# First eight units of a recurrent attention and feed-forward kernel: loads, state copies and hand order rearranged

## The chip, the core and the metric

The kernel runs on one core of a Trainium2 chip. The metric is the time of one execution on the device in microseconds (us). One execution was also recorded by the hardware profiler; its own span, from the first to the last instruction, is a little shorter than the time that is reported for it.

## What is computed

The first half is a linear recurrence per batch and head (4 batches, 8 heads, 768 steps, head size 48). The second half is a feed-forward block with a SiLU over all 3072 tokens (384 to 2048 to 384). All inputs and the output are 32-bit floats.

```python
for t in range(S):
    cur = np.einsum('bhd,bhe->bhde', u[None] * kt, vt)
    y[:, :, t] = np.einsum('bhd,bhde->bhe', rt, state + cur)
    state = w[None, :, :, None] * state + np.einsum('bhd,bhe->bhde', kt, vt)
...
h = x @ w_in
g = h * (1.0 / (1.0 + np.exp(-h)))
return (g @ w_out)
```

## The kernel before

**Units and stages.** The 768 steps are cut into 6 chunks of 128. A unit is one chunk of one batch: 24 units, numbered with the batch running fastest, so units 0 to 3 are the first chunk, units 4 to 7 the second. For a unit the kernel loads r, k and v (one request each of 192 KB, `ld`), transposes r and k on TensorE (`turn`, letter T, into one of two PSUM tiles `att`), multiplies them on VectorE with powers of w (`rT` and `kT`), forms the products of all pairs of steps (`product`, A; two units at once from unit 4 on, `product_pair`, A45), masks them on VectorE (`masked`, am), multiplies with v (`outputs_y`, Y, of which y16 is the sum with the bonus term on VectorE) and brings y into transposed form (yT on TensorE, xT on ScalarE). The bonus term is made on GpSimd (ku, ru, vu) with one sum on VectorE (rd).

**The state.** Between chunks a state per batch is kept twice, in 32 bits (`st`) and in 16 bits (`st16`, shown as stb). `outputs_s` (S) makes a chunk's contribution in a PSUM tile `sp`. In the first chunk, `state` only copies it out, in two halves of 48 rows each, each half once as stb and once as st. In later chunks VectorE adds it to the decayed old state (`decayed_state`, sd, on GpSimd), and `state16` (stb) makes the 16-bit copy on GpSimd. `decayed_k` (kc, GpSimd) is what S reads.

**Feed-forward.** When the units of a chunk are done, w_in is applied in pieces (`l1_mm`, L, into a PSUM tile `hps`, and `l1_silu`, G, on ScalarE) and then w_out (`l2_mm`, into `ops`). A piece of chunk 0 has six multiplications and ends in one G of 512 columns. The word L2.8 means: the pair of batches that starts at 2, columns of w_in from 128 times 8 on. H0 to H3 are such pieces of chunk 1. The tiles hps, sp, yp, yT and ops share four PSUM slots; a new one waits for the oldest to be read.

**What sets the order.** Nothing is rescheduled: each engine runs its instructions in the order in which the program writes them, and waits on semaphores where it needs another engine's result. For the first eight units this order is a list of words in the string `order`, worked off from left to right: a letter and a unit, such as T4, kT4, st1, or a number and a star in front, such as 10*T0, which puts that many idle multiplications (`spin`) on TensorE ahead of the step. lnw, eK and lamK make the powers of w, mx makes the second mask (`cross_mask`), i_q and i_o request quarters of w_in and w_out from GpSimd's queue. After the list a loop takes units 6 and 7, then 8 and 9, and so on, and puts pieces of feed-forward work (`fill`) between their steps.

**First loads.** Requests go out on the queues of SyncE (SP) and ScalarE (ACT) in program order. Ahead of the list stand w in two parts, u spread over all rows (`u_bc`), w as a row (`w_row`), and r, k and v of units 0 to 3; v of unit 0 and k of unit 1 go out on ACT, the others on SP.

Of the kernel before, what the change touches and what calls it, by code (L numbers as in the profile page):

```python
# [15 lines left out]
def kernel(  # L16
# [11 lines left out]
    nc = tc.nc  # L28

    B, H, S, D = r.shape  # L30
    C = 128
# [10 lines left out]
    HC = C // 2  # L42
# [7 lines left out]
    def unit(i):  # L50
        return divmod(i, B)
# [10 lines left out]
    rin = [big.tile([128, H, 64], FP, name=f"rin{i}") for i in range(NIN)]  # L62
    kin = [big.tile([128, H, 64], FP, name=f"kin{i}") for i in range(NIN)]
    vin = [big.tile([128, H, D], FP, name=f"vin{i}") for i in range(NIN)]
# [6 lines left out]
    def ld(i, dst, src, eng=nc.sync):  # L71
        sc, b = unit(i)
        eng.dma_start(
            out=dst[i % NIN][:, :, 0:D],
            in_=src[b, :, sc * C:sc * C + C, :].rearrange("h t d -> t h d"))

    def load(i):
        if i >= NU:
            return
        for dst, src in ((rin, r), (kin, k), (vin, v)):  # L80
            ld(i, dst, src)
# [11 lines left out]
    def columns(eng, dst, src, j):  # L93
        eng.dma_start(out=dst[64 * j:64 * j + D, :],
                      in_=bass.AP(tensor=src.tensor, offset=D * j, ap=[[1, D], [PW, NP]]))
# [6 lines left out]
    nc.vector.memset(idle, 0.0)  # L102
    columns(nc.sync, wpT, w, 1)
    columns(nc.scalar, wpT, w, 0)
    nc.scalar.dma_start(out=u_bc, in_=bass.AP(tensor=u.tensor, offset=0,
                                              ap=[[0, 128], [D, H], [1, D]]))
    nc.scalar.dma_start(out=w_row, in_=bass.AP(tensor=w.tensor, offset=0, ap=[[0, 1], [1, HD]]))
    for i in range(B):
        for dst, src in ((rin, r), (kin, k), (vin, v)):
            by_act = (i == 0 and dst is vin) or (i == 1 and dst is kin)  # L110
            ld(i, dst, src, nc.scalar if by_act else nc.sync)
    nc.vector.memset(ones, 1.0)
    for i in range(B):
        nc.vector.memset(rin[i][:, :, D:64], 0.0)
# [1 line left out]
    for b in range(B):  # L116
# [10 lines left out]
    maskM = cst.tile([128, C], FP)  # L127
    nc.gpsimd.memset(maskM, 1.0)
    nc.gpsimd.affine_select(
        out=maskM, in_=maskM, compare_op=ALU.is_ge, fill=0.0,  # L130
# [3 lines left out]
    maskX = cst.tile([128, C], FP)  # L134
# [6 lines left out]
    eK = cst.tile([PR, NP, C], FP)  # L141
    lamR = cst.tile([PR, NP, C], FP)
    lamK = cst.tile([PR, NP, C], FP)
    lnw_bc = cst.tile([128, HD], FP)
    lamC = cst.tile([128, H, D], FP)
# [39 lines left out]
        nc.scalar.preload_act_table_set("silu_and_others")  # L185

    def cross_mask():
        nc.scalar.copy(out=maskX[0:HC, :], in_=maskM[HC:C, :])
        nc.scalar.copy(out=maskX[HC:C, :], in_=maskM[0:HC, :])

    live = {}

    def L(i):
        return live.setdefault(i, {})

    def bonus_products(i):
        bonus_ku(i)
        bonus_rku(i)
# [10 lines left out]
    def decayed_k(i):  # L209
        nc.gpsimd.tensor_tensor(out=kc[i % NIN][:, :, 0:D], in0=kin[i % NIN][:, :, 0:D],  # L210
                                in1=lamC, op=ALU.mult)

    def bonus_sum(i):
        L(i)["rku"] = wrk.tile([128, H], FP, name="rku")
        nc.vector.tensor_reduce(out=L(i)["rku"], in_=L(i)["rku_f"],  # L215
                                axis=mybir.AxisListType.X, op=ALU.add)

    def bonus_v(i):
        L(i)["vu"] = wrk.tile([128, H, D], FP, name="vu")
        nc.gpsimd.tensor_tensor(out=L(i)["vu"], in0=vin[i % NIN],  # L220
                                in1=L(i)["rku"].unsqueeze(2).broadcast_to([128, H, D]),
                                op=ALU.mult)

    def crossed(i):
        return i >= B and i % 2 == 1
# [47 lines left out]
    def product_pair(i):  # L273
        a = [next_att().rearrange("p j (g c) -> p j g c", g=NP) for _ in range(2)]
        for e in range(2):
            L(i + e)["a"] = a[e]
        for s0, c0 in ((0, 0), (HC, HC)):
            for p in range(NP):
                for e in range(2):
                    rT, kT = L(i + e)["rT"], L(i + e)["kT"]  # L280
                    o0 = s0 if e == 0 else HC - s0
                    for j, r0 in ((0, 0), (1, 64)):
                        nc.tensor.matmul(a[e][o0:o0 + HC, j, p, c0:C],  # L283
                                         kT[r0:r0 + D, p, s0:s0 + HC],
                                         rT[r0:r0 + D, p, c0:C],
                                         start=True, stop=True)

    def masked(i):
        am = L(i)["am"] = wrk.tile([128, 2, NP, C], F16, name="am")
        nc.vector.tensor_tensor(  # L290
            out=am.rearrange("p h g c -> p (h g) c"), in0=L(i)["a"].rearrange("p h g c -> p (h g) c"),
            in1=(maskX if crossed(i) else maskM).unsqueeze(1).broadcast_to([128, H, C]), op=ALU.mult)
# [27 lines left out]
    def outputs(i):  # L320
        outputs_y(i)
        outputs_s(i)

    def decayed_state(i):
        sc, b = unit(i)
        if 0 < sc < NCH - 1:
            L(i)["sdec"] = wrk.tile([PR, NP, PW], FP, name="sdec", bufs=4)
            nc.gpsimd.tensor_tensor(out=L(i)["sdec"], in0=st[b],  # L328
                                    in1=wCT.unsqueeze(2).broadcast_to([PR, NP, PW]), op=ALU.mult)

    def evict_y(i):
        L(i)["y16"] = wrk.tile([128, H, D], F16, name="y16")
        nc.vector.tensor_tensor(out=L(i)["y16"], in0=L(i)["y"], in1=L(i)["vu"], op=ALU.add)  # L333

    def state(i):
        sc, b = unit(i)
        if sc == NCH - 1:
            return
        sps = L(i)["sps"]
        for p0, c0 in ((0, 0), (64, D)):  # L340
            dst = st[b][p0:p0 + D, :, c0:c0 + D]
            src = sps[p0:p0 + D, :, c0:c0 + D]
            if sc:
                nc.vector.tensor_tensor(out=dst, in0=src,
                                        in1=L(i)["sdec"][p0:p0 + D, :, c0:c0 + D], op=ALU.add)
            else:
                nc.scalar.copy(out=st16[b][p0:p0 + D, :, c0:c0 + D], in_=src)  # L347
                nc.scalar.copy(out=dst, in_=src)

    def state16(i):  # L350
        sc, b = unit(i)
# [74 lines left out]
    def fill(n):  # L426
        for _ in range(n):
            if fillers:
                fillers.pop(0)()
# [14 lines left out]
    def piece(word, f):  # L444
# [16 lines left out]
        "lr": lambda i: ld(i, rin, r), "lk": lambda i: ld(i, kin, k), "lv": lambda i: ld(i, vin, v),  # L461
    }
    order = """
        lnw eK lamK pads lr4 lk4 lv4 lr5 lk5 lv5 lr6 lk6 lv6 lr7 lk7 lv7 10*T0 ku0 kT0 rT0 v160
        ru0 5*A0 rd0 ku1 am0 T1 wb v161 ru1 lnwb lamC kT1 rT1 1*Y0 vu0 rd1 T2 i_q0 y160 A1 vu1
        yT0 xT0 v162 ku2 am1 kT2 rT2 ru2 4*Y1 y161 2*A2 yT1 xT1 i_q1 rd2 vu2 v163 T3 am2 ku3 kT3
        rT3 Y2 L0.0 y162 ru3 A3 i_q2 L0.2 G0.0 yT2 G0.2 xT2 rd3 am3 vu3 kc0 Y3 L0.4 G0.4 y163
        kc1 L0.6 G0.6 yT3 kc2 S0 st0 xT3 i_q3 kc3 L2.0 G2.0 L2.2 G2.2 S1 st1 L2.4 G2.4 L2.6 G2.6
        ku4 mx S2 st2 L0.8 G0.8 L0.10 G0.10 S3 st3 ru4 T4 kT4 rT4 v164 r164 L2.8 G2.8 L2.10
        G2.10 rd4 ku5 i_o0 vu4 T5 kT5 rT5 r165 v165 A45 ru5 kc4 sd4 L0.12 G0.12 am4 L0.14 G0.14  # L470
        am5 kc5 rd5 vu5 sd5 Y4 S4 y164 L2.12 G2.12 st4 Y5 S5 y165 L2.14 G2.14 st5 yT4 xT4 stb4
        stb5 i_o1 T6 kT6 rT6 yT5 xT5 ku6 ru6 i_o2 kc6 v166 r166 H0 H1 H2 T7 kT7 rT7 i_o3 H3 r167
        v167 ku7 ru7 kc7 sd6 sd7
    """
    for word in order.split():
        if "*" in word:
            n, word = word.split("*")
# [18 lines left out]
    for i in range(B + 2, NU, 2):  # L496
        sc, b = unit(i)
        nxt = range(i + 2, min(i + 4, NU))
        product_pair(i)
        if i > B + 2:  # L500
            for n in nxt:
                bonus_products(n)
                decayed_k(n)
        masked(i)
        masked(i + 1)
        if i == B + 2:
            for n in (i, i + 1):
                bonus_sum(n)
                bonus_v(n)
            for n in nxt:  # L510
                bonus_products(n)
                decayed_k(n)
        fill(4)
        outputs(i)
        evict_y(i)
        turn_y_dma(i)
        state(i)
        state16(i)
        fill(2)
        outputs(i + 1)  # L520
        evict_y(i + 1)
        turn_y_dma(i + 1)
        state(i + 1)
        state16(i + 1)
        if b:
            fillers.extend((first(sc) if sc > 1 else rest_first(sc)) + second(sc))
        fill(2)
        for n in nxt:
            turn(n)
            decay(n)  # L530
        load(i + B)
        load(i + 1 + B)
        for n in nxt:
            bonus_sum(n)
            cast_v(n)
            bonus_v(n)
            decayed_state(n)
        for n in nxt:
            fill(2)
            cast_r(n)  # L540
        fill(4)
# [31 lines left out]
```

## Time and profile before

| what | value |
|---|---|
| time, median of 3 runs | 198.1 us (198.0 to 199.08) |
| the profiled execution | 198.3 us, span 196.6 us |
| PE busy | 182.9 us, 93% of the span |
| POOL, ACT, DVE busy | 120.5, 109.8, 97.8 us |
| granted TensorE clock, mean | 0.998 |
| first product of unit 0 on PE | starts at 9.02 us |
| first w_out work on PE (L407) | starts at 52.07 us |

PE is TensorE, PEld its weight loads, DVE is VectorE, ACT is ScalarE, POOL is GpSimd, SP is SyncE. A row of a timeline gives the start in us, the length in us, the engine, the line of the kernel, the operation, output and inputs, shape and count; in brackets stands how long the engine was idle before and what released it. A row of the chain of waits gives start, length and what the end was waiting for. In the chain of waits, PE has 76% of the span, each other engine 6% or less.

### The profile page before, as it was taken

How to read it: one execution, taken by the hardware profiler on the slowest of the kernel's cores; microseconds unless marked ns; L12 is line 12 of the kernel's file. 1: busy time of each engine (PE TensorE's matmuls, PEld its weight loads, DVE VectorE, ACT ScalarE, POOL GpSimd, SP SyncE). 2: the span in 40 equal slices, each digit the busy share in tenths (PEclk: the TensorE clock that was granted, in tenths of full speed). 3: DMA queues.
4: the chain of work that ended last, by engine and by line, in shares of the span. 5: the costliest groups of instructions: out<-in, count | busy, mean ns of one | idle time of the engine just before them, and what ended most of it. 6: DMA issues, size and time to landing. Idle time of an engine off the chain costs nothing.

```text
span 196.6 us, 5505 instructions
## 1 busy us (share of the span) xinstructions
PE 182.9 (93%) x2250; PEld 119.9 (61%) x2250; DVE 97.8 (50%) x172; ACT 109.8 (56%) x223; POOL 120.5 (61%) x159
## 2 busy tenths in 40 slices
PE   7697868789989999999999999999999999999992
PEld 2365757667756787665556665556755657644561
DVE  6389603692683772782782773664564355100121
ACT  4672479968543286056794076792286781089200
POOL 8598993779999968929919829839739230000000
PEclk9999999999999999999999999999999999999999
DMA  3999999968939549259149268176287201410022
GB/s 78 238 207 204 202 182 202 217 126 110 137 72 204 162 88 195 90 129 228 28 80 223 63 151 193 23 148 157 63 179 162 42 3 40 120 43 0 0 80 80
DMA packets 90122, 24.33 MB, mean 124 GB/s; under 512 B 83313, under 2 KB 90098, under 8 KB 90098
## 3 DMA queue, kind: packets, MB, share of 16 engines
q1 hardware_dynamic: 83952, 20.26, 47.1%
q0 software_dynamic: 3712, 3.15, 11.1%
q10 hardware_dynamic: 2434, 0.59, 1.4%
q8 instruction: 17, 0.28, 0.6%
q14 instruction: 7, 0.06, 0.1%
HBM read 20.65 MB, written 4.72 MB: 129 GB/s over the span
## 4 chain that ended last, share of the span: by engine, by line
PE 76%; ACT 6%; DVE 6%; POOL 5%; DMA 3%; issue 2%; SPq 0%; POOLq 0%; DVEq 0%
PE ops L407 32%; PE hps L386 26%; PE att L283 6%; PE att L242 5%; DMA kin<-in_k_dram 3%; PE att L270 2%; DVE am L290 2%; ACT gT L394 2%; PE yp L305 2%; PE yp L300 1%; PE sp L317 1%; DVE rT L248 1%; DVE kT L248 1%; ACT stb L347 1%; POOL ku L202 1%
## 5 line engine op out<-in xcount | busy, mean ns | idle before, releaser
L386 PE MATMUL hps<-xT,win 128*128 128x256 f16 (+1 forms) x384 | 67.7, 326 | 3.0 <-ACT xT L375 2.4
L407 PE MATMUL ops<-wout,gT 128*128 128x384 f16 x384 | 66.4, 326 | 0.0
L394 ACT ACTIVATE gT<-hps 128x512 f16<-128x512 f32 x96 | 55.4, 598 | 18.7 <-PE hps L386 16.3
L386 PEld LDWEIGHTS <-win 128*128 128x128 f16 x384 | 35.8, 98 | 25.4 <-issue 3.2
L407 PEld LDWEIGHTS <-gT 128*128 128x128 f16 x384 | 36.2, 98 | 23.3
L220 POOL TENSOR_TENSOR vu<-vin,rku 128x384 f32<-128x384 f32 x24 | 19.8, 829 | 31.2 <-DVE rku L215 27.8
L413 ACT COPY osb<-ops 128x384 f32<-128x384 f32 x20 | 9.6, 480 | 45.1 <-PE ops L407 45.1
L290 DVE TENSOR_TENSOR am<-att,maskM 128x1024 f16<-128x1024 f32 x14 | 17.1, 1225 | 34.9 <-PE att L283 33.5
L202 POOL TENSOR_TENSOR ku<-kin,u_bc 128x384 f32<-128x384 f32 x24 | 24.1, 1006 | 2.3 <-DMA kin<-in_k_dram 2.0
L206 POOL TENSOR_TENSOR rku_f<-rin,ku 128x384 f32<-128x384 f32 x24 | 24.1, 1002 | 1.8
L210 POOL TENSOR_TENSOR kc<-kin,lamC 128x384 f16<-128x384 f32 x24 | 24.0, 1001 | 0.0
L248 DVE TENSOR_TENSOR kT<-att,lamK 112x512 f32<-112x512 f32 x24 | 16.4, 682 | 14.2 <-PE att L242 14.2
L333 DVE TENSOR_TENSOR y<-yp,vu 128x384 f16<-128x384 f32 x24 | 13.3, 555 | 15.0 <-POOL ku L202 4.6
L248 DVE TENSOR_TENSOR rT<-att,lamR 112x512 f32<-112x512 f32 x24 | 16.4, 684 | 7.2 <-ACT gT L394 4.0
L283 PE MATMUL att<-rT,kT 48*64 48x128 f32 (+1 forms) x640 | 16.5, 248 | 1.3 <-DVE rT L248 1.3
L283 PEld LDWEIGHTS att<-rT,kT 48*64 48x64 f32 x640 | 14.7, 133 | 4.9 <-issue 3.1
L415 DVE COPY osb<-ops 128x384 f32<-128x384 f32 x4 | 2.2, 556 | 22.4 <-PE ops L407 22.4
L328 POOL TENSOR_TENSOR sdec<-st,wCT 112x384 f32<-112x384 f32 x16 | 13.2, 827 | 0.0
L263 ACT CAST rT<-rT 112x512 f16<-112x512 f32 x20 | 12.5, 623 | 0.4 <-DVE rT L248 0.3
L229 ACT CAST v<-vin 128x384 f16<-128x384 f32 x24 | 11.5, 513 | 2.2 <-DMA vin<-in_v_dram 2.2
L215 DVE TENSOR_REDUCE rku<-rku_f 128x8 f32<-128x384 f32 x24 | 12.3, 542 | 0.3 <-POOL rku_f L206 0.3
L290 DVE TENSOR_TENSOR am<-att,maskX 128x1024 f16<-128x1024 f32 x10 | 12.1, 1213 | 0.0
(60 smaller groups left out, 167.2 us busy)
## 6 DMA issues: line engine op xcount, KB each, us to landing
rin<-in_r_dram SPq DMA_DIRECT2D x24, 192.0 KB, 3.9
out_dram<-osb SPq DMA_DIRECT2D x24, 192.0 KB, 2.1
kin<-in_k_dram SPq DMA_DIRECT2D x23, 192.0 KB, 3.8
vin<-in_v_dram SPq DMA_DIRECT2D x23, 192.0 KB, 3.8
win<-in_moe_w_in_dram POOLq DMA_DIRECT2D x4, 384.0 KB, 6.1
wout<-in_moe_w_out_dram POOLq DMA_DIRECT2D x4, 384.0 KB, 5.1
xT<-y SPq DMA_TRANSPOSE x18, 2.3
u_bc<-in_u_dram ACTq DMA_DIRECT2D x1, 192.0 KB, 4.5
```

Of the source, the lines that this page charges most:

```text
L202: nc.gpsimd.tensor_tensor(out=L(i)["ku"], in0=kin[i % NIN][:, :, 0:D], in1=u_bc, op=ALU.mult)
L206: nc.gpsimd.tensor_tensor(out=L(i)["rku_f"], in0=rin[i % NIN][:, :, 0:D], in1=L(i)["ku"], op=ALU.mult)
L210: nc.gpsimd.tensor_tensor(out=kc[i % NIN][:, :, 0:D], in0=kin[i % NIN][:, :, 0:D], in1=lamC, op=ALU.mult)
L220: nc.gpsimd.tensor_tensor(out=L(i)["vu"], in0=vin[i % NIN], in1=L(i)["rku"].unsqueeze(2).broadcast_to([128, H, D]), op=ALU.mult)
L248: nc.vector.tensor_tensor(out=L(i)[key].rearrange("p g (y t) -> p y g t", y=2), in0=L(i)["t"][0:PR, :, x], in1=lam.rearrange("p g (y t) -> ...
L283: nc.tensor.matmul(a[e][o0:o0 + HC, j, p, c0:C], kT[r0:r0 + D, p, s0:s0 + HC], rT[r0:r0 + D, p, c0:C], start=True, stop=True)
L290: nc.vector.tensor_tensor(out=am.rearrange("p h g c -> p (h g) c"), in0=L(i)["a"].rearrange("p h g c -> p (h g) c"), in1=(maskX if crossed ...
L328: nc.gpsimd.tensor_tensor(out=L(i)["sdec"], in0=st[b], in1=wCT.unsqueeze(2).broadcast_to([PR, NP, PW]), op=ALU.mult)
L333: nc.vector.tensor_tensor(out=L(i)["y16"], in0=L(i)["y"], in1=L(i)["vu"], op=ALU.add)
L386: nc.tensor.matmul(hps[:, f, :], win[:, q, (ft + f) * 128:(ft + f + 1) * 128], xts[sc][:, q, b0:b0 + nb, :].rearrange("p b t -> p (b t)"), ...
L394: nc.scalar.activation(out=gts[sc][:, ft:ft + m, b0 * C:(b0 + nb) * C], in_=hpss[b0, ft], func=AF.Silu)
L407: nc.tensor.matmul(opss[b], gts[sc][:, ft, b * C:(b + 1) * C], wout[:, ft, :], start=(ft == 0), stop=(ft == NFT - 1))
```

## The change

Lines are those of the kernel before and after. On loading: r of unit 0 stays the first load on SP, k of unit 0 becomes the first on ACT, ahead of u_bc, then v of unit 0 and w_row; all loads of units 1 to 3 go to SP. The copies of the first state are split, stb on ACT and st on DVE; the second mask is made on DVE. In the list, xT3 and the mask stand ahead of S0 and st0; T4, kT4, rT4 move from behind st3 to behind S0; each S of units 1 to 3 stands between two pieces L; the first i_o, T5, ru5, rd5, A45, yT4, T6, T7 and the other i_o get other places; three spins fewer stand ahead of T0 and A0; rT0 stands ahead of kT0. kc6, kc7, sd6 and sd7 leave the list, and in the first round of the loop vu of units 6 and 7 comes ahead of kc and sd of the same unit, with rd6 at the end of the list.

```diff
--- before.py
+++ after.py
@@ -102,13 +102,14 @@
     nc.vector.memset(idle, 0.0)
     columns(nc.sync, wpT, w, 1)
     columns(nc.scalar, wpT, w, 0)
+    ld(0, rin, r)
+    ld(0, kin, k, nc.scalar)
     nc.scalar.dma_start(out=u_bc, in_=bass.AP(tensor=u.tensor, offset=0,
                                               ap=[[0, 128], [D, H], [1, D]]))
+    ld(0, vin, v, nc.scalar)
     nc.scalar.dma_start(out=w_row, in_=bass.AP(tensor=w.tensor, offset=0, ap=[[0, 1], [1, HD]]))
-    for i in range(B):
-        for dst, src in ((rin, r), (kin, k), (vin, v)):
-            by_act = (i == 0 and dst is vin) or (i == 1 and dst is kin)
-            ld(i, dst, src, nc.scalar if by_act else nc.sync)
+    for i in range(1, B):
+        load(i)
     nc.vector.memset(ones, 1.0)
     for i in range(B):
         nc.vector.memset(rin[i][:, :, D:64], 0.0)
@@ -185,8 +186,8 @@
         nc.scalar.preload_act_table_set("silu_and_others")
 
     def cross_mask():
-        nc.scalar.copy(out=maskX[0:HC, :], in_=maskM[HC:C, :])
-        nc.scalar.copy(out=maskX[HC:C, :], in_=maskM[0:HC, :])
+        nc.vector.tensor_copy(out=maskX[0:HC, :], in_=maskM[HC:C, :])
+        nc.vector.tensor_copy(out=maskX[HC:C, :], in_=maskM[0:HC, :])
 
     live = {}
 
@@ -345,7 +346,7 @@
                                         in1=L(i)["sdec"][p0:p0 + D, :, c0:c0 + D], op=ALU.add)
             else:
                 nc.scalar.copy(out=st16[b][p0:p0 + D, :, c0:c0 + D], in_=src)
-                nc.scalar.copy(out=dst, in_=src)
+                nc.vector.tensor_copy(out=dst, in_=src)
 
     def state16(i):
         sc, b = unit(i)
@@ -461,16 +462,16 @@
         "lr": lambda i: ld(i, rin, r), "lk": lambda i: ld(i, kin, k), "lv": lambda i: ld(i, vin, v),
     }
     order = """
-        lnw eK lamK pads lr4 lk4 lv4 lr5 lk5 lv5 lr6 lk6 lv6 lr7 lk7 lv7 10*T0 ku0 kT0 rT0 v160
-        ru0 5*A0 rd0 ku1 am0 T1 wb v161 ru1 lnwb lamC kT1 rT1 1*Y0 vu0 rd1 T2 i_q0 y160 A1 vu1
+        lnw eK lamK pads lr4 lk4 lv4 lr5 lk5 lv5 lr6 lk6 lv6 lr7 lk7 lv7 8*T0 ku0 rT0 kT0 v160
+        ru0 4*A0 rd0 ku1 am0 T1 wb v161 ru1 lnwb lamC kT1 rT1 1*Y0 vu0 rd1 T2 i_q0 y160 A1 vu1
         yT0 xT0 v162 ku2 am1 kT2 rT2 ru2 4*Y1 y161 2*A2 yT1 xT1 i_q1 rd2 vu2 v163 T3 am2 ku3 kT3
         rT3 Y2 L0.0 y162 ru3 A3 i_q2 L0.2 G0.0 yT2 G0.2 xT2 rd3 am3 vu3 kc0 Y3 L0.4 G0.4 y163
-        kc1 L0.6 G0.6 yT3 kc2 S0 st0 xT3 i_q3 kc3 L2.0 G2.0 L2.2 G2.2 S1 st1 L2.4 G2.4 L2.6 G2.6
-        ku4 mx S2 st2 L0.8 G0.8 L0.10 G0.10 S3 st3 ru4 T4 kT4 rT4 v164 r164 L2.8 G2.8 L2.10
-        G2.10 rd4 ku5 i_o0 vu4 T5 kT5 rT5 r165 v165 A45 ru5 kc4 sd4 L0.12 G0.12 am4 L0.14 G0.14
-        am5 kc5 rd5 vu5 sd5 Y4 S4 y164 L2.12 G2.12 st4 Y5 S5 y165 L2.14 G2.14 st5 yT4 xT4 stb4
-        stb5 i_o1 T6 kT6 rT6 yT5 xT5 ku6 ru6 i_o2 kc6 v166 r166 H0 H1 H2 T7 kT7 rT7 i_o3 H3 r167
-        v167 ku7 ru7 kc7 sd6 sd7
+        kc1 L0.6 G0.6 yT3 xT3 mx S0 st0 kc2 T4 kT4 rT4 i_q3 kc3 L2.0 G2.0 S1 L2.2 G2.2 st1 ku4
+        v164 L2.4 G2.4 S2 L2.6 G2.6 st2 ru4 r164 L0.8 G0.8 S3 L0.10 G0.10 st3 rd4 ku5 T5 kT5 rT5
+        i_o0 vu4 L2.8 G2.8 ru5 A45 rd5 L2.10 G2.10 am4 r165 v165 L0.12 G0.12 kc4 L0.14 G0.14 am5
+        vu5 L2.12 G2.12 sd4 kc5 Y4 S4 y164 st4 L2.14 G2.14 sd5 Y5 S5 yT4 xT4 y165 st5 i_o1 yT5
+        xT5 H0 stb4 T6 kT6 rT6 stb5 ku6 i_o2 H1 v166 r166 ru6 H2 i_o3 H3 T7 kT7 rT7 ku7 v167
+        r167 ru7 rd6
     """
     for word in order.split():
         if "*" in word:
@@ -501,12 +502,19 @@
             for n in nxt:
                 bonus_products(n)
                 decayed_k(n)
-        masked(i)
-        masked(i + 1)
-        if i == B + 2:
-            for n in (i, i + 1):
-                bonus_sum(n)
-                bonus_v(n)
+        if i > B + 2:
+            masked(i)
+            masked(i + 1)
+        else:
+            bonus_v(i)
+            decayed_k(i)
+            decayed_state(i)
+            masked(i)
+            bonus_sum(i + 1)
+            masked(i + 1)
+            bonus_v(i + 1)
+            decayed_k(i + 1)
+            decayed_state(i + 1)
             for n in nxt:
                 bonus_products(n)
                 decayed_k(n)
```

## The prediction

> **What bounds the kernel now.** I read the stretches first, to see which part of the span can still give time.
>
> ```profile
> 0.00:24.00 24.00, 19.24 (x217) 12.26 (x218) 16.76 (x36) 12.10 (x29) 20.12 (x41) 1.00 1.00 185
> 24.00:36.00 12.00, 8.57 (x114) 7.18 (x115) 3.04 (x5) 10.75 (x31) 8.54 (x10) 1.00 1.14 197
> 42.00:58.00 16.00, 14.31 (x231) 11.22 (x228) 9.72 (x18) 10.21 (x21) 15.26 (x19) 1.00 0.69 100
> 58.00:190.00 132.00, 132.00 (x1565) 82.53 (x1563) 62.66 (x105) 72.37 (x137) 72.75 (x87) 1.00 0.48 109
> ```
>
> The columns are stretch, length, busy PE, PEld, DVE, ACT, POOL, clock, DMA. From 58 us on PE never rests, so the end is fixed by when PE gets there and with how much of its work done. Only PE's idle time before 58 us counts. From 24 to 36 us ACT is busy 10.75 of 12 us; from 42 to 58 us POOL 15.26 of 16. Then the chain of waits, which names the holes:
>
> ```profile
> 1.90 5.10 DMA kin<-in_k_dram
> ...
> 9.02 1.19 PE att L270 x16
> ...
> 25.62 0.22 ACT st L348
> 25.86 0.49 ACT xT L375
> 26.39 1.49 PE hps L386 x12
> ...
> 52.52 0.83 POOL sdec L328
> 53.35 0.80 POOL vu L220
> 54.17 0.57 DVE y L333
> 54.78 0.33 PE sp L317 x4
> ```
>
> k of unit 0 arrives at 7.00 and the first product (A0) starts at 9.02; the piece L2.0 waits until 26.39 for xT3, which stands behind four state copies on ACT; S7 waits for y of unit 6, whose vu stands behind four other POOL instructions. The timeline of ACT prices the state copies:
>
> ```profile
> 24.78 0.30 ACT L347 CAST stb<-sp 48x192 f16<-48x192 f32 x1
> 24.98 0.31 ACT L348 COPY st<-sp 48x192 f32<-48x192 f32 x1
> 25.30 0.31 ACT L347 CAST stb<-sp 48x192 f16<-48x192 f32 x1
> 25.52 0.31 ACT L348 COPY st<-sp 48x192 f32<-48x192 f32 x1
> ```
>
> Four copies hold ACT for 1.08 us (24.78 to 25.86). Last, the waits of SP's queue:
>
> ```profile
> SPq L73 <- DMA rin<-in_r_dram: 3.2, 1, 3.2
> ```
>
> A request of SP's stood 3.2 us, until 6.27, for r of unit 0 to land, though it asks for v of unit 1: in the built program hardware requests share eight semaphores in turn, and the one that reuses a semaphore waits for its last user. The changed program has such a wait on ACT.
>
> [...] the second stb copy on ACT waits for DVE, and each st copy on DVE for ACT. So the split makes a hand-over, not a parallel pair. For the DVE copy out of PSUM no row exists; the nearest is the add of the same shape (L344, 0.35 us). [...] I take 0.35, with 0.25 and 0.42 as bounds. [...]
>
> **The change, part by part.** I put each engine's new order on the clock with the durations of the rows, an instruction starting when its engine is free and what it waits for has ended plus 0.03 us.
>
> *First loads.* r0 stays first on SP, k0 becomes first on ACT. Section 6 has 3.9 us from issue to landing for the median load: r0 issued at 1.42 lands at 5.3, not about 6.3; k0 somewhat later, 5.5, not 7.00. Bounds for r0: 4.7 and 6.25 (no gain). u_bc falls behind k0, v0 and u_bc land near their old times, k1 goes to SP and lands about 9 us, before its use at 10.24; later SP requests only move in a queue with slack. But w_row's request on ACT now comes ninth among the hardware requests and must wait for r0's semaphore. lnw stands behind it on ACT. So: 5.3, plus w_row's issue 0.67 (its own row), so lnw at 6.0 where it was at 3.69, a shift of 2.35. lamR 3.99 to 5.27 becomes 6.3 to 7.6, lamK ends at 8.1; on DVE rT0 (7.6) then kT0 (8.2 to 8.9), A0 at 8.95. The gain of 1.5 us in k0 shrinks to 0.05. Bounds for A0: 8.2 to 9.9. The eight pads and v16 of unit 0 slip on ACT to about 10.3, still before Y0 at 11.6. Three fewer spins (8 and 4 for 10 and 5) were waiting time: nothing.
>
> *xT3 first, T4 early, masks to DVE.* The order from A0 to Y3 is the same. xT3 now follows G0.6 at 24.8 and ends 25.26; L2.0 starts at 25.3 for 26.39, and T4 (0.6) fills the wait: a gain of 1.1 plus 0.6. The masks (0.61 on ACT) run at 23.5 on DVE, in its hole of 8.17 us.
>
> *State copies, hand-over.* One state takes ACT 0.31, DVE 0.35, ACT 0.31, DVE 0.35 and four hops: 1.45 us in all, of which ACT is held 1.03. Before it was held 1.08: nothing is freed. And DVE's part comes later than ACT's. Walk: L2.0 25.3, S1, L2.2, L2.4 to 27.4, S2, L2.6 to 28.25. st1 runs 27.43 to 28.84 and its PSUM slot lets L0.8 start at 28.87 (0.6 idle); L0.10 waits for G2.6 (0.3). ACT goes on without a hole: v164 (0.42), G2.4 and G2.6 (1.1), st2 from 29.9 (1.0), r164 (0.5), G0.8 and G0.10 (1.1), so st3 starts at 32.43 and DVE's last copy ends at 33.84. Behind it on DVE stand rd4, kT5, rT5: 33.8 plus 0.46, 0.61 and 0.69, end 35.55. T5 itself is long done (31.25). So A45 goes on at 35.6, where it was at 35.78, with one piece (L2.10, 0.65) less done. PE idles 3.5 us there. Balance: the 1.7 won has become 0.45 lost.
>
> *After A45.* Product to 37.1, four pieces at 0.65 to 39.7, Y4 to 40.1. S4's slot is freed by G0.12, which stands on ACT behind G2.10, r165, v165 and two vx (38.4 to 40.5, then 0.6): S4 at 41.1, 1.0 idle. L2.14, Y5, S5, yT4, then 0.4 for y16 of unit 5 and 0.7 for its xT: H0 at 44.0 for 43.30, and T6 (0.6) still to come: 1.3 behind. T6, H1 to H3 (2.6 with H0), T7 to 47.86; T7 now comes last, so kT7 and rT7 (1.3) are bare: A67 goes on at 49.2 for 47.40, 1.8 behind.
>
> *The first round of the loop.* vu6 no longer stands behind kc6, kc7, sd6, sd7 (3.6 us of POOL); rd6 (now ahead of am6 on DVE) ends near 49.6, vu6 near 51, before y16 of unit 6. The wait of 1.03 us at S7 (53.75 to 54.78) goes: 0.8 behind. The later i_o requests on POOL (0.81 each) start within 1 us of their old times against a first need of w_out at 52 us; i_o1 ahead of stb costs only POOL slack.
>
> *Sum.* 0 + 0.45 + 0.85 + 0.5 − 1.0 = +0.8 us. The same walk of the old order reaches A67 0.4 us ahead of the trace; the new order has as many small losses, so the difference of two walks is 1.2. I take +1.1 on the span of 196.6. That run is given at 198.3, the median of the runs at 198.1: 199.2. What this kernel's measurement can tell from no change is about 0.5%, 1 us, so the forecast lies on that edge.
>
> **Rivals.** *The hand-over does not bind* (ends on the other side): if ACT and DVE read their halves at once, ACT is held 0.6 per state instead of 1.03, four times 0.4 is 1.6 us before A45, which moves from 35.6 to 34: 1.1 − 1.6 = −0.5, and with r0 landing at 4.7 (0.6) −1.1, 197.0. It decides if a state takes under 0.75 us from the first copy's start to the last one's end. Against it: the waits in the order. *The first loads win nothing*: [...] r0 lands at 6.25 as before; the chain behind w_row then gives A0 9.9, +0.9 more: 200.1. Against it: u_bc no longer shares r0's first microseconds. *The front gain comes through*: r0 at 4.7 and w_row's issue at 0.4 give A0 8.1, 198.3. *The change does not do what it says*: the built order has every move, so only cancelling is left, and that is inside the forecast.
>
> **How the numbers follow.** Forecast 0.60, own range 198.2 to 200.4: 0.24 within 0.5%, 0.36 slower. Hand-over not binding 0.20: 0.14 faster, 0.06 within. No win at the front 0.14: slower. Full win at the front 0.06: within. Sums: faster 0.14, same 0.36, slower 0.50. The range 197.0 to 201.0 takes in the copy's bounds (0.4 us either way) and A0's.
>
> **What would show it.** Right: lnw on ACT after 5.5, A0 within 0.5 of 9.0, L2.0 near 25.3, ACT and DVE alternating through each state, A45 held by rT5 until 35 or later, A67 held by rT7, no wait of S7 for vu. Wrong: A0 before 8.2, or A45 going on before 34.5; then the change is no slower. A PE wait past 58 us would break the whole frame.

## The result and the profile after

| | before | after |
|---|---|---|
| time, median | 198.02 us (five runs, 198.0 to 199.08) | 201.26 us (five runs, 200.51 to 204.3) |
| ratio to before | 1 | 1.0144, 95% interval 1.0106 to 1.0181 |
| granted TensorE clock, mean of each run | 0.998 in the profiled one | 0.980, 0.983, 0.991, 0.991, 0.991 |
| profiled execution | span 196.6 us | span 202.5 us |

The change costs 2.9 us by the ratio, 3.2 by the medians, where 1.1 was forecast. Runs more than 1.5% above the fastest of their kernel are left out of the ratios, here the one of 204.3 us. That longest run is also the profiled one, so what it shows is read below only where another kernel's profile or the times support it. The granted clock is the share of its full speed at which TensorE was allowed to run.

The stretches first, in the same columns as before (stretch, length, busy PE, PEld, DVE, ACT, POOL, clock, DMA):

```profile
0.00:24.00 24.00, 19.21 (x214) 12.20 (x215) 17.03 (x37) 11.98 (x29) 20.40 (x41) 1.00 1.01 188
24.00:36.00 12.00, 8.11 (x100) 6.16 (x97) 7.31 (x13) 8.09 (x20) 5.81 (x7) 1.00 1.18 199
42.00:58.00 16.00, 13.64 (x203) 11.13 (x202) 8.51 (x15) 12.00 (x23) 10.71 (x14) 0.93 0.57 75
58.00:190.00 132.00, 132.00 (x1616) 83.34 (x1615) 65.55 (x111) 75.08 (x142) 78.02 (x93) 1.00 0.48 108
```

From 58 us on PE again never rests: the loss lies ahead of 58 us. From 24 to 36 us ACT is busy 8.09 us where it was 10.75, and yet PE is busy for less time, 8.11 us for 8.57. The new thing is the clock of 0.93 from 42 to 58 us, where it was 1.00. The chain of waits, asked for 20 to 62 us, shows what leads there:

```profile
23.65 0.83 DVE maskX L189
24.49 2.73 DVE maskX L190
...
34.59 0.20 ACT stb L348
34.81 0.36 DVE st L349
35.20 0.32 ACT stb L348
35.55 0.37 DVE st L349
35.94 0.55 DVE rku L216
36.52 0.69 DVE kT L249
37.21 0.61 DVE rT L249
37.87 2.83 PE att L284 x58
40.69 4.44 PE hps L387 x24
```

ACT and DVE hand each state to and fro (st3: stb, st, stb, st), then DVE makes rd4, kT5 and rT5, and only then can A45 go on, at 37.87. PE's timeline has this wait as 3.36 us, where it was 1.02. First the kernel before, then the kernel after:

```profile
35.78 1.55 PE L283 MATMUL att<-rT,kT 48*64 48x128 f32 x60 [1.02 <-DVE rT L248]
```

```profile
37.87 2.83 PE L284 MATMUL att<-rT,kT 48*64 48x128 f32 x60 [3.36 <-DVE rT L249]
```

And what follows is slow: 2.83 us for products that took 1.55 before, 4.44 us for four pieces L that take 2.6 to 2.8 at full clock (2.79 further on in the same profile, from 55.86). The kernel after in steps of 2 us:

```profile
36.00:38.00 2.00, 0.14 (x4) 0.14 (x8) 1.78 (x3) 0.13 (x1) 1.42 (x2) 0.84 1.15 224
38.00:40.00 2.00, 2.00 (x46) 2.00 (x50) 0.55 (x1) 0.00 (x0) 2.00 (x3) 0.50 1.09 216
42.00:44.00 2.00, 2.00 (x11) 1.40 (x10) 1.09 (x1) 1.85 (x4) 1.41 (x2) 0.50 0.03 5
44.00:46.00 2.00, 1.70 (x26) 1.47 (x24) 0.45 (x1) 1.96 (x5) 0.00 (x0) 0.96 0.88 96
```

The clock falls to 0.50 inside the hole (the time in which PE stands idle ahead of A45), at 37.34, and stays there until 44.17, 6.83 us, with PE busy from 37.87 on. At the front, the timeline of ACT answers to SP's wait of before:

```profile
5.02 0.49 ACTq L110 DMA_DIRECT2D w_row<-in_w_dram  x1
5.62 0.20 ACT L161 ACTIVATE lnwT<-wpT 112x4 f32<-112x4 f32 x1 [3.54 <-DMA w_row<-in_w_dram]
```

w_row's request now holds lnw until 5.62, as the order said it would.

### The profile page after: what moved, and what is told of

It is laid out like the page before. It is cut to its first block, busy times and chain, and to the rows that moved or that the text cites. A ratio compares the mean times of both kernels' runs of the same rounds, so it can differ in the third digit from the quotient of the medians.

```text
span 202.5 us, 5500 instructions
## 1 busy us (share of the span) xinstructions
PE 186.1 (92%) x2247; PEld 121.7 (60%) x2247; DVE 104.2 (51%) x182; ACT 107.3 (53%) x213; POOL 120.4 (59%) x159
## 4 chain that ended last, share of the span: by engine, by line
PE 78%; DVE 6%; DMA 6%; ACT 4%; POOL 2%; issue 1%; ACTq 0%; POOLq 0%; DVEq 0%
PE ops L408 31%; PE hps L387 29%; PE att L284 8%; PE att L243 4%; DMA win<-in_moe_w_in_dram 4%; DMA u_bc<-in_u_dram 3%; PE yp L306 2%; ACT gT L395 2%; PE yp L301 2%; DVE maskX L190 1%; PE sp L318 1%; POOL ku L203 1%; DVE rT L249 1%; DVE st L349 1%; DVE y L334 1%
## 5 line engine op out<-in xcount | busy, mean ns | idle before, releaser
L387 PE MATMUL hps<-xT,win 128*128 128x256 f16 (+1 forms) x384 | 69.8, 332 | 3.8 <-DVE st L349 2.1
L387 PEld LDWEIGHTS <-win 128*128 128x128 f16 x384 | 36.6, 100 | 27.7 <-issue 2.4
L284 PE MATMUL att<-rT,kT 48*64 48x64 f32 (+1 forms) x640 | 17.8, 259 | 4.4 <-DVE rT L249 4.4
L284 PEld LDWEIGHTS att<-rT,kT 48*64 48x64 f32 x640 | 15.9, 141 | 8.0 <-DVE rT L249 4.9
L354 POOL CAST stb<-st 112x384 f16<-112x384 f32 x16 | 8.0, 508 | 9.0 <-DVE st L345 9.0
```

Source lines behind the costliest of these rows:

```text
L284: nc.tensor.matmul(a[e][o0:o0 + HC, j, p, c0:C], kT[r0:r0 + D, p, s0:s0 + HC], rT[r0:r0 + D, p, c0:C], start=True, stop=True)
L387: nc.tensor.matmul(hps[:, f, :], win[:, q, (ft + f) * 128:(ft + f + 1) * 128], xts[sc][:, q, b0:b0 + nb, :].rearrange("p b t -> p (b t)"), ...
```

## The experiments

Unless another base is named, a kernel is the one after with one edit. "Full clock" below means the runs of a kernel whose mean clock is 0.996 or more, which leaves room for the fall of the clock behind PE's last work (from 195.7 us on in the profile before).

**First explanation: the masks.** The two mask copies took 0.30 us each on ACT and 0.83 and 2.73 on DVE, with st0 behind them. The author's guess, which no trace had shown, was that the form of the instruction matters; a sum over one element does the copy's work in another form. Three kernels: the sums, the masks back on ACT, and only the masks moved in the kernel before.

```diff
-        nc.vector.tensor_copy(out=maskX[0:HC, :], in_=maskM[HC:C, :])
-        nc.vector.tensor_copy(out=maskX[HC:C, :], in_=maskM[0:HC, :])
+        for o, i in ((0, HC), (HC, 0)):
+            nc.vector.tensor_reduce(out=maskX[o:o + HC, :], in_=maskM[i:i + HC, :].unsqueeze(2),
+                                    axis=mybir.AxisListType.X, op=ALU.add)
```

> The kernel after, with the two mask copies still on DVE at the same place, but written as a sum over one element each (a tensor_reduce of 64x128 fp32) in place of a copy. The output is the same. Theory (the copies stood 0.83 and 2.73 us [...]; st0 behind them held A45): each takes about 0.25 us, st0's first DVE copy starts before 25.5 us instead of 27.26, A45 goes on near 35.6 instead of 37.87, the PE hole ahead of it stays under 3.5 us, time 199.2 (197.0 to 198.0 was before), range 198.6 to 199.9. Rival 1 (the masks are not what matters, the split of the state copies and the late T7 cost more than was worked out): 201, A45 still after 37. Rival 2 (DVE is simply slow on such a tile, any form): each sum takes over 0.8 us and the time stays at 201.

Measured: 202.19 us, ratio to before 1.0183 (1.0143 to 1.0223). The timelines of DVE, first of the variant with sums, then of the kernel after:

```profile
23.67 0.57 DVE L190 TENSOR_REDUCE maskX<-maskM 64x128 f32<-64x128 f32 x2
```

```profile
23.65 0.83 DVE L189 COPY maskX<-maskM 64x128 f32<-64x128 f32 x1
24.49 2.73 DVE L190 COPY maskX<-maskM 64x128 f32<-64x128 f32 x1
```

Same tile, same place, GpSimd busy with its products in both: 0.57 us for two sums, 3.56 for two copies. What makes the copies the slower ones, the profile does not show. A45 goes on at 36.13, with the hand-over as forecast, and PE still waits 3.36 us ahead of it. The time did not improve: the theory that the masks made the loss falls. In this variant's profile, too, the clock falls to 0.50, from 37.33 to 40.75, and its six runs have mean clocks of 0.975 to 0.991.

```diff
-        nc.vector.tensor_copy(out=maskX[0:HC, :], in_=maskM[HC:C, :])
-        nc.vector.tensor_copy(out=maskX[HC:C, :], in_=maskM[0:HC, :])
+        nc.scalar.copy(out=maskX[0:HC, :], in_=maskM[HC:C, :])
+        nc.scalar.copy(out=maskX[HC:C, :], in_=maskM[0:HC, :])
```

> The kernel after, with the two mask copies back on ACT (0.30 us each before), at the same place in the order. Theory [...]: they take 0.30 each, the first st copies move 0.6 us back on ACT instead of 2.2 on DVE, A45 goes on near 36.2, time 199.6, range 198.9 to 200.3; so within 0.5 us above the variant with sums. Rival 1 (masks do not matter): 201. Rival 2 (DVE slow in any form): 199.6 here but 201 for the variant with sums.

Measured: 202.7 us (1.017 to 1.025 of before), 0.5 above the sums (the intervals overlap), and both 3 us above what was expected. A45 goes on at 36.81, again after 3.36 us of waiting, and the clock is 0.50 from 37.45 to 40.87.

The kernel before, with cross_mask as in the kernel after and mx at another place:

```diff
-        rT3 Y2 L0.0 y162 ru3 A3 i_q2 L0.2 G0.0 yT2 G0.2 xT2 rd3 am3 vu3 kc0 Y3 L0.4 G0.4 y163
+        rT3 Y2 L0.0 y162 ru3 A3 i_q2 L0.2 G0.0 yT2 G0.2 xT2 rd3 am3 vu3 kc0 Y3 L0.4 G0.4 y163 mx
...
-        ku4 mx S2 st2 L0.8 G0.8 L0.10 G0.10 S3 st3 ru4 T4 kT4 rT4 v164 r164 L2.8 G2.8 L2.10
+        ku4 S2 st2 L0.8 G0.8 L0.10 G0.10 S3 st3 ru4 T4 kT4 rT4 v164 r164 L2.8 G2.8 L2.10
```

> The kernel before, with only its two mask copies moved from ACT to DVE, as copies, right behind y of unit 3, where DVE is idle for 8.17 us. Theory: they again take over 3 us together (23.6 to 27.2)[...], but nothing stands behind them on DVE until 31 us, so nothing is late; ACT is 0.6 us shorter before A45: 197.5, range 197.2 to 198.1. Rival (the copies slow GpSimd or its transfers, and that is what costs the time): a GpSimd product between 23.6 and 28 takes 1.3 us or more, or w_in's piece comes later, and the time is 199 or more.

Measured: 197.42 us, ratio 0.997 (0.9953 to 0.9988). The move of the masks by itself gains 0.6 us. The copies took 0.22 and 0.94 us here, not the 3 us expected. Of the nine profiles with these copies on DVE, seven have about these lengths; in two they held DVE for over 3 us, in the kernel after (0.83 and 2.73) and in the variant with the old first round (below), whose DVE was busy for 3.38 of the 3.41 us from 24.00 on, with two instructions. Here and with eight spins the first copy started about 0.1 us ahead of the third of GpSimd's three products kc, in the kernel after about 0.2 us behind its start. So the start against that product goes with the length in these three profiles; that it made the difference was not tried.

**Second explanation: the clock.** If the hole on PE lowers the clock, idle multiplications in the hole must raise it. Eight, then fourteen, both on the kernel after:

```diff
-        i_o0 vu4 L2.8 G2.8 ru5 A45 rd5 L2.10 G2.10 am4 r165 v165 L0.12 G0.12 kc4 L0.14 G0.14 am5
+        i_o0 vu4 L2.8 G2.8 ru5 8*A45 rd5 L2.10 G2.10 am4 r165 v165 L0.12 G0.12 kc4 L0.14 G0.14 am5
```

> The kernel after, with eight matmuls of zeros (about 1.7 us of PE, results unused) ahead of A45, inside the hole of 3.4 us in which PE waits for rT5. Theory (the hole sends the granted clock to 0.5 from 37.7 to 44.1 us, a loss of its own on top of the wait): PE's idle stretch falls under 2 us, the clock stays at 1.00 to 60 us, A45 goes on at the same 37.9, time 199.7, range 199.0 to 200.4, against 201.3 for the kernel after. Rival (the clock falls whatever PE does there, or the pieces after A45 have slack for it): 201.0 to 201.6, clock under 0.99.

Measured: 201.0 us; but the clock had not stayed up. PE still stood 1.45 us ahead of A45, the clock was 0.50 from 37.45 to 40.87 in the profile, and the mean clock was under 0.996 in five of six runs. The sixth, at 1.000, took 199.63 us, the others 200.64 to 204.08. So the edit was too small to decide, and its one run at full clock pointed on.

```diff
-        i_o0 vu4 L2.8 G2.8 ru5 A45 rd5 L2.10 G2.10 am4 r165 v165 L0.12 G0.12 kc4 L0.14 G0.14 am5
+        i_o0 vu4 L2.8 G2.8 ru5 14*A45 rd5 L2.10 G2.10 am4 r165 v165 L0.12 G0.12 kc4 L0.14 G0.14 am5
```

> The kernel after, with fourteen matmuls of zeros (about 3.0 us of PE, results unused) ahead of A45 in place of the eight of the run before, which left an idle stretch of 1.45 us and a clock of 0.5 from 37.4 to 40.8. Theory (on top of the wait that was forecast, the hole makes the granted clock fall to 0.5 for one stretch or more of about 3.4 us, and that is the part of the loss the forecast missed): PE idles under 0.6 us there, the clock stays at 1.00, and with A45 where it was the time is that of the one run of the eight-matmul variant that had clock 1.000, 199.6; range 199.2 to 200.2, mean clock 0.997 or more. Rival (the clock falls for another reason, or the slower pieces lie beside other waits): 201.0 or more with or without the clock.

Measured: 200.0 us (nine runs, 199.54 to 202.15), ratio to before 1.010 (1.0067 to 1.0133), mean clock 0.997 to 1.000 in all nine. PE's timeline:

```profile
31.98 3.18 PE L158 MATMUL zs<-idle 128*128 128x512 f16 x14
35.09 0.44 PE L284 MATMUL att<-rT,kT 48*64 48x128 f32 x4
35.69 1.55 PE L284 MATMUL att<-rT,kT 48*64 48x128 f32 x60 [0.16 <-DVE rT L249]
```

and its stretches of 2 us:

```profile
36.00:38.00 2.00, 2.00 (x68) 1.85 (x58) 1.26 (x2) 0.00 (x0) 2.00 (x4) 1.00 1.06 210
38.00:40.00 2.00, 2.00 (x25) 1.81 (x23) 1.65 (x2) 1.92 (x4) 2.00 (x3) 1.00 0.67 130
```

Work that computes nothing makes the kernel 1.3 us faster (201.26 to 200.0): A45 goes on when rT5 is there, at 35.69, and takes 1.55 us. The direction is clear, as the clock held in all nine runs; the size is less so, since the intervals of the two ratios overlap (1.0067 to 1.0133, and 1.0106 to 1.0181 for the kernel after). What is left at full clock is 2.0 us over the kernel before; the clock is a part that was missing from the forecast.

The runs with low clock show the price. A mean clock of 0.991 over 199 us is, as an estimate, 3.6 us at half rate (0.009 times 199 times 2), one stretch of the 3.41 us that the profiles show; 0.983 is two. Medians by the number of such stretches, in brackets the number of runs (three runs with three stretches are left out):

| kernel | none | one | two |
|---|---|---|---|
| all state copies on ACT (below) | 196.76 (16) | 197.92 (2) | 198.81 (2) |
| that, old first round (below) | 196.67 (14) | 197.63 (5) | 198.36 (3) |
| kernel before with the split (below) | 199.87 (3) | 200.75 (1) | 201.81 (1) |

A stretch goes with 0.7 to 1.2 us. An estimate from the clock of 0.50 is that PE at full load would lose half of 3.41, 1.7 us; that part of the slow work lies over waits that are there anyway is likely, not shown. Nor is it known where the stretches of runs without a profile lay, or what else differed in them.

**The parts of the change.** The kernel after with the state copies back on ACT; the kernel before with the split alone; the kernel before with the new first loads.

```diff
-                nc.vector.tensor_copy(out=dst, in_=src)
+                nc.scalar.copy(out=dst, in_=src)
```

> The kernel after, with the copies of the new state back on ACT (all four copies of a state on ACT, as before); everything else of the change stays. Theory (the hand-over between ACT and DVE is what keeps A45 back, since st3's DVE copies stand ahead of rT5): ACT is held 1.08 us per state instead of 1.03 with no wait between, rd4, kT5 and rT5 run on DVE as soon as T5 and POOL allow, A45 goes on about 2 to 3 us sooner, near 33.5, the hole shrinks under 1.5 us and the clock stays at 1.00: 196.3, range 195.6 to 197.2. Rival 1 (T7's place and the first loads cost as much as the hand-over): 198 to 199. Rival 2 (ACT becomes the bound again, as the piece L2.0 behind four copies was before): 198.5 or more.

Measured: 196.86 us, ratio to before 0.9944 (0.9922 to 0.9966). PE's timeline around A45:

```profile
31.94 0.43 PE L284 MATMUL att<-rT,kT 48*64 48x128 f32 x4
32.64 1.55 PE L284 MATMUL att<-rT,kT 48*64 48x128 f32 x60 [0.26 <-DVE rT L249]
```

A45 goes on at 32.64, 3.05 us ahead of the variant with fourteen idle multiplications, and the wait is 0.26 us. One line undone turns a kernel that is 3.2 us slower than before into one that is 1.1 us faster: the split costs 4.4 us (201.26 to 196.86), 3.2 of them at full clock (200.0 to 196.76). The line takes away two things at once, the hand-over within a state and the st copies that stand ahead of kT5 and rT5 on DVE; which of them costs how much was not separated.

The reverse edit of that line in the kernel before:

```diff
-                nc.scalar.copy(out=dst, in_=src)
+                nc.vector.tensor_copy(out=dst, in_=src)
```

> The kernel before, with only the split: the copy of the new state on DVE, the one to fp16 on ACT. Theory (hand-over, with st3 on DVE ahead of kT5 and rT5): the state takes 1.45 us, L2.0 still waits behind stb on ACT, A45 moves later by 1.5 to 2 us, PE's hole ahead of it grows from 1.4 to about 3 us: 199.6 with a clock of 1.00, up to 201 where the clock falls. Rival (the two engines' parts lie beside each other, as the forecast's first rival had it): ACT is freed by 0.5 us per state, 197.4.

Measured: 200.31 us, ratio 1.0101 (1.0056 to 1.0146), 199.87 at full clock. The split alone loses 2.0 us by the ratio, 2.3 by the medians, and the clock fell in three of its six runs. The profiled one has, besides 38.15 to 44.97, a stretch at the front, 7.43 to 10.84, which the edit does not touch: not every stretch comes from the hole ahead of A45.

```diff
+    ld(0, rin, r)
+    ld(0, kin, k, nc.scalar)
     nc.scalar.dma_start(out=u_bc, in_=bass.AP(tensor=u.tensor, offset=0,
                                               ap=[[0, 128], [D, H], [1, D]]))
+    ld(0, vin, v, nc.scalar)
     nc.scalar.dma_start(out=w_row, in_=bass.AP(tensor=w.tensor, offset=0, ap=[[0, 1], [1, HD]]))
-    for i in range(B):
-        for dst, src in ((rin, r), (kin, k), (vin, v)):
-            by_act = (i == 0 and dst is vin) or (i == 1 and dst is kin)
-            ld(i, dst, src, nc.scalar if by_act else nc.sync)
+    for i in range(1, B):
+        load(i)
```

> The kernel before, with only the first loads in the order of the kernel after (r and k of unit 0 first on two queues, w_row last on ACT; the spins stay 10 and 5). Theory: A0 starts 0 to 0.6 us sooner, but w_row's request waits for r of unit 0 and w_in's first piece lands later, so A3 starts within 0.2 us of where it was: 198.1, range 197.7 to 198.5. Rival (the front gain comes through): 197.5 or less. Rival (the later lnw and k1 cost): 199 or more.

Measured: 198.35 us, ratio 1.0024 (1.0006 to 1.0042). PE's timeline has A0 where it was (9.02 before):

```profile
8.98 1.16 PE L271 MATMUL att<-rT,kT 48*128 48x128 f32 x16 [0.89 <-DVE rT L249]
```

The new loads alone win nothing. The clock fell in three of these 22 runs, and in none of the 46 runs of the kernel before beside them.

**What is left in the order**, on the variant with the state copies on ACT. First T7 between H1 and H2:

```diff
-        xT5 H0 stb4 T6 kT6 rT6 stb5 ku6 i_o2 H1 v166 r166 ru6 H2 i_o3 H3 T7 kT7 rT7 ku7 v167
+        xT5 H0 stb4 T6 kT6 rT6 stb5 ku6 i_o2 H1 v166 r166 ru6 T7 kT7 rT7 H2 i_o3 H3 ku7 v167
```

> The variant with all state copies on ACT (196.9), with one more edit: the transposes and decays of unit 7 stand between H1 and H2 on PE, not behind H3. Theory (T7 last leaves kT7 and rT7 bare: PE waits 1.02 us for rT7 after the first products of A67): two pieces of 0.7 us now lie over them, the wait of 1.02 goes, and as nothing else moves: 195.8, range 195.5 to 196.3. Rival (r and k of unit 7 or a free att buffer are not there before, or the pieces behind wait for ACT's silus): a wait of about 1 us appears ahead of T7 or H2 instead: 196.5 to 197.

T7 stood ahead of H3 in the kernel before and behind it in the kernel after; here it stands ahead of H2.

Measured: 195.51 us, ratio to before 0.9872 (0.9835 to 0.9909): the fastest kernel of this study. A67, first without and then with the edit:

```profile
46.62 1.55 PE L284 MATMUL att<-rT,kT 48*64 48x128 f32 x60 [1.02 <-DVE rT L249]
```

```profile
45.62 1.59 PE L284 MATMUL att<-rT,kT 48*64 48x128 f32 x64
```

The wait of 1.02 us is gone, and 1.35 us of time with it; at full clock it is 1.3 (196.76 to 195.44).

Then the old first round of the loop:

```diff
-        xT5 H0 stb4 T6 kT6 rT6 stb5 ku6 i_o2 H1 v166 r166 ru6 H2 i_o3 H3 T7 kT7 rT7 ku7 v167
-        r167 ru7 rd6
+        xT5 H0 stb4 T6 kT6 rT6 stb5 ku6 i_o2 kc6 H1 v166 r166 ru6 H2 i_o3 H3 T7 kT7 rT7 ku7 v167
+        r167 ru7 kc7 sd6 sd7
...
-        if i > B + 2:
-            masked(i)
-            masked(i + 1)
-        else:
-            bonus_v(i)
-            decayed_k(i)
-            decayed_state(i)
-            masked(i)
-            bonus_sum(i + 1)
-            masked(i + 1)
-            bonus_v(i + 1)
-            decayed_k(i + 1)
-            decayed_state(i + 1)
+        masked(i)
+        masked(i + 1)
+        if i == B + 2:
+            for n in (i, i + 1):
+                bonus_sum(n)
+                bonus_v(n)
```

> The variant with all state copies on ACT (196.9), with the first round of the loop as in the kernel before: kc6, kc7, sd6 and sd7 issued on GpSimd ahead of the loop, and the bonus sums and vu of units 6 and 7 after both masks. Theory (the new round is what took away the wait of S7 for y of unit 6, as forecast): that wait comes back, 0.8 to 1.0 us: 197.7, range 197.3 to 198.2. Rival (A67 is reached at another time against GpSimd's work, so vu6 is no longer late in either order): no wait, 196.9, within 0.3.

Measured: 197.03 us, ratio 0.9947 (0.9928 to 0.9965), at full clock 196.67 against 196.76. No wait of S7 for y comes back, though A67 goes on at 47.39, the same time as in the kernel before. The rival holds for this variant: GpSimd's timeline has vu of units 6 and 7 at

```profile
51.88 1.61 POOL L221 TENSOR_TENSOR vu<-vin,rku 128x384 f32<-128x384 f32 x2 [0.53 <-DVE rku L216]
```

where the chain before has vu6 at 53.35. GpSimd had even been idle for 0.53 us. What brought it forward is not separated: the w_out request placed ahead of stb4 and the earlier A45 are both in this variant.

Last, w_row's request behind k of unit 0, on top of T7's edit, and then the casts of unit 5 as well:

```diff
     ld(0, kin, k, nc.scalar)
+    nc.scalar.dma_start(out=w_row, in_=bass.AP(tensor=w.tensor, offset=0, ap=[[0, 1], [1, HD]]))
     nc.scalar.dma_start(out=u_bc, in_=bass.AP(tensor=u.tensor, offset=0,
                                               ap=[[0, 128], [D, H], [1, D]]))
     ld(0, vin, v, nc.scalar)
-    nc.scalar.dma_start(out=w_row, in_=bass.AP(tensor=w.tensor, offset=0, ap=[[0, 1], [1, HD]]))
```

> The variant with the state copies on ACT and unit 7's transposes between H1 and H2, with one more edit: w_row's request stands right behind k of unit 0 on ACT, ahead of u_bc and v. Theory (as ninth hardware request it waits for r of unit 0 and holds lnw, lamR and lamK behind it, so A0 waits 1.4 us for kT0): lnw runs before 4.5 us instead of 5.7, A0 starts near 7.6 instead of 8.6; but ku0 waits for u_bc, 0.5 us later, and the w_in pieces land when they land, so of the 1.0 won at A0 at most half is left at A3: 195.4, range 195.1 to 195.9. Rival (k of unit 0, or u_bc by way of vu0, sets the pace): 195.8, as without the edit.

Measured: 197.49 us, ratio 0.9945 (0.9922 to 0.9968), 2 us slower than without the edit. lnw runs at 3.64 and A0 starts at 7.71, as expected. But PE then waits 1.20 us ahead of Y0, and its stretches show what follows:

```profile
10.00:12.00 2.00, 0.80 (x10) 0.41 (x9) 2.00 (x3) 1.89 (x5) 1.92 (x3) 0.83 1.03 204
12.00:14.00 2.00, 2.00 (x31) 1.94 (x30) 1.75 (x4) 0.94 (x1) 1.98 (x3) 0.50 1.09 217
```

The clock is 0.50 from 11.32 to 18.15, two stretches of 3.41 us. Of 22 runs, 14 have a mean clock of 0.982 or 0.983 (median 197.65), three are at full clock (195.69, 195.77, 196.69): even those gain nothing over 195.44. An earlier start came with a hole and a fall of the clock behind it; that the hole made the fall was not tried here, as no idle multiplications were put into it.

```diff
-        i_o0 vu4 L2.8 G2.8 ru5 A45 rd5 L2.10 G2.10 am4 r165 v165 L0.12 G0.12 kc4 L0.14 G0.14 am5
+        i_o0 vu4 L2.8 G2.8 ru5 A45 rd5 L2.10 G2.10 am4 L0.12 G0.12 r165 v165 kc4 L0.14 G0.14 am5
```

> The variant before this one, with one more edit: the casts of r and v of unit 5 stand behind the silu of L0.12 on ACT instead of ahead of it. Theory (S4 waits 0.94 us because the silu that frees its PSUM slot stands behind four copies of 2.1 us on ACT): S4's wait goes, but the copies move by 0.6 us towards Y5 and xT4: 0.2 us won, 195.2, range 194.9 to 195.6. Rival (Y5 then waits for vx of unit 5): 195.4 or more. If it holds, this is the fastest version, 1.4 % under the kernel before.

Measured: 197.25 us (0.9934 to 0.997 of before). S4's wait of 0.94 us goes and one of 0.47 for y comes at the next piece. The medians differ by 0.24 us, where 0.2 was expected, but both lie about 2 us above what was expected of them, under the low clock (one or two stretches in 19 of 21 runs here), so the edit stays unproven.

## Why the prediction was right in direction and too small

**The frame** held in part. No PE wait lies past 58 us. But "Only PE's idle time before 58 us counts" took PE's rate for given, and every PE row came from a profile at clock 1.00. This is the step that failed. The working names the hole ("PE idles 3.5 us there") and prices it as 3.5 us, not as 3.5 us and then slower work. The missing term is about 1.3 us (201.26 against 200.0 with the hole filled). In the profiles the clock fell from 1.00 to 0.50, for 3.41 or 6.83 us, and not only where PE had stood idle for most of the time: with eight spins PE was busy 1.96 of the 3.41 us ahead of the fall, with w_row moved 2.57. That the time still lies near the upper end of the stated range, 197.0 to 201.0 (the ratio gives 200.9), is luck: the range had room for the copies and for A0, not for the clock.

**First loads**, forecast 0: lnw at 5.62 for 6.0, A0 at 8.57 for 8.95, and A3 at 20.09 for 20.07 before, since one piece then waited 0.41 us for w_in. Right in the sum; alone, the new loads lose 0.4 us (interval 0.1 to 0.8).

**xT3, T4, masks**: L2.0 at 25.32 for 25.3. The masks were costed at nothing because DVE had a hole; that was wrong for the row (1.2 to 3.6 us, where ACT had taken 0.61) and no measured loss for the time: undoing their form gained nothing. The hole of DVE was read from the kernel before, where no st copy stood behind it.

**Hand-over**: ACT and DVE alternate, the DVE copy takes 0.34 to 0.36 us, and A45 goes on at 35.69, 35.84 and 36.13 in the profiles with fourteen spins, eight spins and sums, for 35.6. Right, and the first rival, that it does not bind, is out. Why two engines do not read at once here was not shown; the waits are. In the kernel after, DVE stands idle for 0.38 us until ACT's stb releases the second st of a state (27.99, 30.31, 32.87, 35.55). And the second stb waits for the first st, though the two halves of a state lie in different rows (0 to 47 and 64 to 111), as ACT's timeline with fourteen spins shows:

```profile
25.47 0.31 ACT L348 CAST stb<-sp 48x192 f16<-48x192 f32 x1 [0.42 <-DVE st L349]
```

Whether the two halves could be copied at once was not tried. What the working did not bring out is how much the split costs beside the rest: set off against the gain ahead of it, it appeared as 0.45 us, where undoing it is worth 3.2 at full clock.

**After A45**, with fourteen spins: S4 at 41.30 for 41.1, H0 at 44.22 for 44.0, A67 at 49.67 for 49.2. T7's late place, forecast as 0.5 of the balance, has a price of 1.3 against a place ahead of H2; against its old place, ahead of H3, it was not measured.

**First round**: S7's wait is gone, as forecast, but the cause given is not shown. With the old round, tried where all state copies are on ACT, it does not come back.

**The sum.** In the one pair of profiles at full clock the spans are 197.8 and 196.6, +1.2 for +1.1. By the medians (200.0 and 197.96) it is +2.0, interval 1.3 to 2.6; the 0.8 us between the two readings is the spread of single executions (the profiled one with fourteen spins, 199.54, is the fastest of its nine) and was not traced to a step. So: about +2.0 for the order, +1.3 for the clock, against 1.1 and nothing.

## What to carry to other kernels

A hole on TensorE may not be over when it ends (behind 3.36 us of waiting in the kernel after and 1.20 with w_row moved, the clock was 0.50 for 6.83 us in all): price the work behind it at half rate for one stretch or two as well, and look at the mean clock of every run before explaining a median. A split of copies from one PSUM tile over two engines was a chain here (0.38 us idle ahead of the second st, 0.42 or more ahead of the second stb), not a pair; walk to what stands behind the last link. And a hole of an engine in the old profile is free only if nothing new has been put behind it.

## What the runs showed of the hardware

- The clock was 0.50 for 3.41 us (the profiles with sums, masks on ACT and eight spins, one stretch each) or 6.83 (the kernel after, w_row moved). With fourteen idle multiplications on zeros in the hole the mean clock was 0.997 to 1.000 in all nine runs; with eight it was 0.996 or more in one of six.
- Times between two changes of the clock were whole multiples of 3.41 us: 3.41 and 6.83 for the stretches above, 27.31 (eight) between the end of the first stretch and the next fall with the split alone, 10.84 to 38.15. In the kernel after the first fall, at 37.34, came 30.72 us (nine) after the first clock on record.
- What makes the clock fall is not settled. In the 3.41 us ahead of a fall PE was busy 0.57 (the kernel after), 0.65 (masks on ACT), 1.20 (sums), 1.60 and 1.77 (the split alone), 1.96 (eight spins), 1.99 and 2.57 us (w_row moved, with and without the casts). Yet the clock was 1.00 in and behind windows of that length with 1.65 us busy (the kernel after, from 27.12 to 30.53) and 1.61 (the new loads alone, from 24.00 to 27.41). So busy time alone does not decide; whether small fp32 products make a difference here was not tried.
- The views say 1.00 where no clock is on record yet (up to 6.62 us in the kernel after). But the eight idle multiplications that start at 1.29 there took 3.59 us, 0.45 each, and the fourteen at 31.98 in the variant with spins 3.18 us, 0.23 each. As an estimate from these two rows, that is half the rate at the very front, too.
- Two fp32 copies of 64x128 between SBUF tiles on VectorE took 0.22 and 0.94 us, or 0.83 and 2.73, beside running GpSimd products, and as `tensor_reduce` 0.28 each.
